# A hand-written order of steps, re-ordered: fused sparse attention and gated MLP on one core

## The chip, the cores and the metric

The kernel runs on one core of a Trainium2 chip. A core has five engines that run side by side: TensorE (PE, matmuls; PEld is its weight load), VectorE (DVE), ScalarE (ACT), GpSimd (POOL) and SyncE (SP, which here only starts transfers). The metric is the device time of one execution in microseconds (us), as the median of several runs.

## The reference, cut to what matters

There are 8 batches, 8 heads, 576 positions and 64 columns per head. The first half of the heads attends to the last 32 positions, the second half to the positions that are congruent modulo 32. The attention's output x then goes through a gated MLP.

```python
scores = scale * np.matmul(q, k.transpose(0, 1, 3, 2))
scores = np.where(masks, scores, -1e9); scores -= scores.max(-1, keepdims=True)
attn = np.exp(scores); attn /= attn.sum(-1, keepdims=True) + 1e-9
x = heads_to_columns(attn @ v)                 # (8, 576, 512)
h = gelu_tanh(x @ w_in)                        # 512 -> 1024
u, v = h[..., :512], h[..., 512:]
v_n = (v - mean(v)) / sqrt(var(v) + 1e-6) * g_ln
v_s = einsum('ts,bsd->btd', w_sg, v_n) + b_sg[None, :, None]
out = x + (u * v_s) @ w_out
```

## The kernel before

The loop runs over the 8 batches. While the MLP of batch b runs, the attention of batch b+1 is worked out beside it, and q, k and v of batch b+2 are loaded. Nothing is ordered by a scheduler at run time: three strings, START (batch 0 with the conversion of the weights), CYCLE (batches 1 to 6) and LAST (batch 7), list some hundred short steps, `emit` (L985) walks the list, and every engine and every DMA queue executes its instructions strictly in the order in which the list issues them. Only the order among steps of one engine matters; steps of different engines meet at semaphores and at buffers that come free.

A word is a step's name, an optional mark and an index: `ug:3` is the gelu of the fourth quarter of u. A trailing `-`, or none with a name in capitals, or `+`, names the batch of an attention step; `=` is a step without a batch. A `^` sets `alt`, which some helpers read: `loads()` (L144) puts a load on ACT's queue instead of SP's, `slow()` (L148) takes DVE instead of POOL, `fast()` (L152) POOL instead of DVE, and `mm_tile`/`at_tile` (L160, L163) swap the two PSUM pools, of two buffers of two banks each. Steps that read none of these ignore the mark.

The steps that matter here, by engine, for a batch in CYCLE:

- PE: `v1`, `v2`, `v` (x times the second half of w_in, 12, 12 and 8 matmuls), `u:0` to `u:3` (24 matmuls each, a PSUM tile each), `SL`, `SS` (scores), `s` (w_sg times the normed v, 28 matmuls a quarter), `PL`, `PS` (transposes of the softmax), `VA`, `PV`, `PW` (times v), `o`, `o2` (the two halves of the output product of a 128-row chunk, 6 matmuls each).
- ACT: `g` (gelu of v), `vh`, `ug` (gelu of u, which frees u's PSUM buffer), `lh` (normed v as high part), `EX` (exp), `sh` (gated product, high part), `XH`, `CL`, `CS` (copies), and the DMA issues `XD` (x to DRAM) and `od` (output). Gelu and exp lie in different activation tables, so an ACT_TABLE_LOAD is put between a gelu and an exp in ACT's order.
- DVE: `ls`, `lm`, `ll` (layer norm), `MK`, `MX`, `SU` (mask, max, sum of the softmax), `sm`, `sl` (gate, low part), `TQ` (transposes), `XL`, `XR`, `os`.
- POOL: `lr` (inverse square root by 14 tiny instructions), `SB`, `ML`.
- SP: loads `LQ`, `LP`, `LV`, `cl`, `wl`, `r`, `rt`.

In START the weights are converted by the chain `cl` (load), `ca`, `cb`, `cc`, `cd`, `ce`, `cf`, `cg`, `ch`, each by an index 0 to 15 over pieces of w_in and w_out; `ce` is one DVE instruction, and with `^` one on ACT and one on POOL. `TP` and `TC` turn the rows of q and k (PE) and copy them from PSUM (ACT).

Of the kernel before, what the change touches and what calls it, by code (L numbers as in the profile page):

```python
# [21 lines left out]


START = """
mk= mp= cl=:3 ca=:3 cl=:1 LP-^:3 cb=:3 cc=:3 ca=:1 cb=:1 cl=:0 cc=:1 cd=:1 cd=:3 cl=:2 TZ-:0
ca=:2 cl=:8 ml= ce=:3 ca=:0 cb=:0 ce=^:1 TP-^:6 TC-:6 cb=:2 TP-^:7 TC-:7 cf=^:1 cg=:1 cc=:2
cd=:2 LP-:0 SS-:3 LP-:1 TZ-:1 ca=:8 cb=:8 ch=:1 cc=:0 cd=:0 cl=:9 ce=^:0 TP-:1 MK-:3 TP-:0 TC-:0
MX-:3 SB-^:3 TC-:1 ce=:2 EX-:3 cf=^:2 LP-^:2 TP-^:2 TC-:2 SL-^:0 MK-:4 ca=:9 TP-^:3 TC-:3 SL-:1
MX-:4 wb= SB-:4 cl=:6 ca=:6 cb=:6 cc=:6 cl=^:4 cc=:8 LZ-:0 wc= wd= we= LZ-:1 wl=:1 MK-:5 MX-:5
cf=^:3 EX-:4 TP-:4 TC-:4 SU-:4 SB-:5 LP:1 SU-:3 cg=:2 ch=:2 cd=:8 TP-:5 cf=:0 wt=:1 TC-:5 SS-^:2  # L30
cd=:6 cg=:3 cl=^:7 EX-:5 ML-:4 SU-:5 TP^:2 TC:2 MK-:2 MX-:2 cg=:0 ch=:0 TZ:0 ce=^:6 LV-:0
ML-^:5 ca=:4 TP:3 TZ:1 TC:3 wh=:1 ch=:3 wm=:1 ca=:7 SB-^:2 PL-:4 CL-:4 PL-^:5 CL-:5 CM-:5 VX-:0
VY-:0 XR-:0 EX-:2 SU-:2 cb=:4 cc=:4 ML-^:2 LP:0 TP^:0 cb=:7 LV-:1 TC:0 XHa-:0 XLa-:0 ce=^:8
cf=:8 TP^:1 TC:1 cb=:9 cc=:9 XHb-:0 XLb-:0 cf=^:6 cl=:5 PS-^:2 CS-:2 ca=:5 XD-:0 SL^:0 SL:1 MK:0
VA-:1 XH-:1 XL-:1 cd=:4 cc=:7 LV-:2 PV-^:2 PW-:2 XH-:2 cd=:9 ce=:9 wo= wp= ML-:3 LP:2 XR-:1 MX:0
PS-:3 CS-:3 cb=:5 SB:0 XD-:1 va:0 vb:0 cl=^:13 TP^:4 TC:4 XL-:2 vc:0 LV-:3 PV-:3 XR-:2 PW-:3
cd=:7 XH-:3 cc=:5 TP^:5 EX:0 ce=:4 cf=^:4 cg=:4 ch=:4 va:1 XL-:3 xt LP:3 vd:0 g:0 XD-:2 vb:1
ce=:7 XR-:3 cf=^:9 ls:0 lr^:0 wl=:0 TP^:6 TC:6 cd=:5 cl=^:15 vc:1 cf=:7 cg=:7 cg=:9 vd:1 TP:7
v^:2 LZ:1 ce=:5 ch=^:9 ca=:13 cf=^:5 TC:7 cg=:6 g:1 LV:1 ls:1 cg=:5 ch=^:5 SS^:3 ch=:6 ch=:7 u:2
MK:3 TC:5 cb=:13 vh XD-:3 cc=:13 TZ+:0 cd=:13 ce=:13 lg= vl g:2 wt=^:0 cf=^:13 wl=^:4 rt cl=:10  # L40
lm:0 lh:0 ls:2 lm:1 wh=:0 lm:2 wm=:0 lr:1 lh:1 ll:0 cg=:8 SS:2 ug:2 lr:2 wl=:2 u^:1 ug:1 wt=^:4
ca=:15 ca=:10 cb=:10 cb=:15 u:0 SU:0 wh=:4 cc=:10 wl=:3 wm=:4 cc=:15 cd=:10 ce=:10 cf=:10 MK:2
wt=:2 LQ+:0 ug:0 wh=:2 wm=:2 cl=^:11 wt=^:3 wh=:3 wm=:3 ML:0 lh:2 ll:2 cg=:13 u:3 ll:1 cd=:15
ca=:11 ce=^:15 cb=:11 cc=:11 PL:0 CL:0 ch=:13 ug:3 MX:3 SB^:3 s:3 cd=:11 ce=:11 cf=:11 cg=:11
CM:0 s^:2 cf=^:15 MX:2 SB^:2 s^:0 ch=^:11 sm:3 sm:2 cl=^:12 ca=:12 TZ+:1 EX:3 SU:3 sh:2 sl:2 s:1
sh:3 cb=:12 ML^:3 LZ:0 cg=:10 cc=:12 VA^:1 cd=:12 LQ+:3 sm:0 ch=:8 cg=:15 cl=:14 ch=^:10 ca=:14
ch=^:15 ce=^:12 cf=:12 sh:0 sl^:0 TQ+:0 cg=:12 LV:0 sm:1 sh:1 sl:1 r cb=:14 cc=:14 EX:2 LQ+:1
VA:0 XR:1 PS:3 CS:3 o:0 o^:1 ch=:12 sl:3 cd=:14 ce=:14 cf=^:14 cg=:14 SU:2 ML^:2 XH:0 XL:0
ch=:14 XH:1 XL:1 LV:3 o^:2 o^:3 o2:2 os:2 XD:1 XR:0 XD:0 o2:0 o2:3 os:3 LV:2 PS^:2 o2:1 PV:3
PW:3 CS:2 od:2 PV:2 od:3 PW:2 TQ+:1 XH:3 LZ+:1 XL:3 XH:2 XR:3 XD:3 os:1 XR:2 XD:2 od:1 LZ+:0  # L50
os:0 od:0 LV+^:0 LQ+:2 LV+:1 XL:2
"""
# [16 lines left out]


# [971 lines left out]
```

## Time and profile before

| | |
|---|---|
| median of 3 runs (lowest, highest) | 584.68 us (584.05, 585.74) |
| the profiled execution | 583.31 us, of which 581.2 us are its span |
| busy: PE, PEld | 539.7 us (93%), 483.2 us (83%) |
| busy: DVE, ACT, POOL | 398.9 (69%), 250.1 (43%), 191.9 us (33%) |
| mean granted TensorE clock | 0.997 of full speed |

The span runs from the first to the last instruction of the profiled execution. Matmuls are pipelined and their ends are modelled, so a busy PE is one that has work under way; what it lacks to the span is time in which it waited.

### The profile page before, as it was taken

The page shows a single profiled execution, that of the slowest core. Times are in us where ns is not written, and L with a number is a line of the kernel's source. Part 1 is how long each engine was busy: PE and PEld are TensorE (multiplying, and loading weights), DVE is VectorE, ACT ScalarE, POOL GpSimd, SP SyncE. Part 2 cuts the span into 40 slices and gives each one's busy share as a digit, 9 for nine tenths or more (in the row PEclk, how much of TensorE's full clock was granted, in tenths as well). Part 3 has the DMA queues.
Part 4 walks back from the last instruction along what each step waited for, and adds up shares of the span by engine and source line. Part 5 has one row for each costly group of instructions (what it writes and reads, how often), then busy time and mean ns, then how long its engine had stood idle before and what let it go on. Part 6 is the DMA issues. An engine that isn't in the chain of part 4 may idle for free.

```text
span 581.2 us, 17089 instructions
## 1 busy us (share of the span) xinstructions
PE 539.7 (93%) x7217; PEld 483.2 (83%) x7217; DVE 398.9 (69%) x692; ACT 250.1 (43%) x371; POOL 191.9 (33%) x447
## 2 busy tenths in 40 slices
...
GB/s 242 179 191 188 128 136 106 180 156 148 184 50 42 185 154 123 42 118 176 173 50 47 184 158 122 42 120 179 172 53 47 186 186 4 1 122 157 1 0 90
DMA packets 253678, 70.08 MB, mean 121 GB/s; under 512 B 237793, under 2 KB 239329, under 8 KB 253602
## 3 DMA queue, kind: packets, MB, share of 16 engines
...
q8 instruction: 56, 0.92, 0.7%
...
## 4 chain that ended last, share of the span: by engine, by line
PE 72%; DVE 7%; POOL 7%; DMA 5%; ACT 5%; issue 3%; ACTq 1%; SPq 0%; POOLq 0%
PE sg L83 21%; PE o L83 17%; PE v L83 11%; PE u L83 10%; POOL nt L83 4%; PE ol L83 3%; PE os L83 3%; PE pts L83 2%; DMA xd<-xs 2%; POOL y L83 2%; PE ptl L83 1%; PE sa L83 1%; ACTq L83 1%; DMA stage<-in_moe_w_in_dram 1%; DVE bnst L83 1%
## 5 line engine op out<-in xcount | busy, mean ns | idle before, releaser
L83 PE MATMUL u<-xt,wih 128*128 128x288 f32 x512 | 105.6, 301 | 8.7 <-ACT u L83 8.3
L83 PE MATMUL sg<-wsh,vg 128*128 128x288 f32 x512 | 113.0, 296 | 0.0
L83 PE MATMUL o<-woh,vg 128*128 128x512 f32 x288 | 95.2, 397 | 0.0
L83 PEld LDWEIGHTS u<-xt,wih 128*128 128x128 f32 x512 | 83.2, 190 | 11.5 <-ACT u L83 9.7
L83 PEld LDWEIGHTS sg<-wsh,vg 128*128 128x128 f32 x512 | 85.6, 188 | 0.5
L83 PE MATMUL v<-wih,xt 128*128 128x512 f32 x256 | 83.9, 398 | 1.0 <-issue 1.0
L83 PE MATMUL u<-xt,wil 128*128 128x288 f32 x256 | 76.3, 298 | 0.8 <-DVE wil L83 0.8
L83 PE MATMUL sg<-wsl,vg 128*128 128x288 f32 x256 | 75.3, 294 | 0.0
L83 ACT ACT_TABLE_LOAD x40 | 51.3, 1283 | 54.9 <-DVE kT L83 23.2
L83 PEld LDWEIGHTS o<-woh,vg 128*128 128x128 f32 x288 | 54.1, 188 | 10.8
L83 PEld LDWEIGHTS v<-wih,xt 128*128 128x128 f32 x256 | 48.0, 188 | 12.2 <-issue 1.6
L83 PE MATMUL o<-wol,vg 128*128 128x512 f32 x144 | 56.3, 391 | 0.0
L83 DVE TENSOR_TENSOR ob<-o,xn 128x512 f32<-128x512 f32 x32 | 22.0, 689 | 45.1 <-PE o L83 44.3
L83 PE MATMUL v<-wil,xt 128*128 128x512 f32 x128 | 50.0, 391 | 0.0
L83 PEld LDWEIGHTS u<-xt,wil 128*128 128x128 f32 x256 | 48.7, 190 | 1.0 <-DVE wil L83 1.0
L83 ACT CAST vg<-gt 128x576 fp32r<-128x576 f32 (+2 forms) x48 | 22.8, 509 | 61.6 <-DVE gt L83 61.5
L83 PEld LDWEIGHTS sg<-wsl,vg 128*128 128x128 f32 x256 | 48.2, 188 | 0.0
L83 DVE TENSOR_TENSOR gt<-sg,u 128x576 f32<-128x576 f32 x32 | 23.6, 740 | 23.5 <-PE sg L83 14.6
L83 DVE BATCH_NORM_STATS2 bnst<-hv 128x6 f32<-128x512 f32 (+1 forms) x40 | 27.0, 676 | 17.4 <-ACT hv L83 17.1
L83 POOL TENSOR_TENSOR sms<-sms,sr 100x576 f32<-100x576 f32 x13 | 15.0, 1156 | 61.5 <-DVE sr L83 61.4
L83 DVE SCALAR_TENSOR_TENSOR vg<-hv,y,vg 128x512 fp32r<-128x512 f32 x32 | 22.5, 748 | 14.3 <-ACT vg L83 14.3
L83 ACT CAST xt<-ol 128x576 fp32r<-128x576 f32 (+2 forms) x17 | 10.3, 611 | 49.5 <-DVE ob L83 23.1
...
## 6 DMA issues: line engine op xcount, KB each, us to landing
xd<-xs ACTq DMA_DIRECT2D x128, 72.0 KB
...
```

What stands on the lines that cost most here:

```text
L83: ins = self.tc.keep_in_program_order(op(*args, **kwargs))
```

## The change

All three lists are written in a new order. Each holds the same steps as before (427, 139 and 72 of them). Some marks differ; those that have an effect are `ce=:1` (all on DVE), and in CYCLE `sl:2` and `ML:3` (now DVE), `CM:0` (now ACT), and the PSUM pools of `s:1` and `s:3`. A new helper `stores()` sends a store on SP's queue where the step is marked: that is `XD-:2` in START and `od:3` in CYCLE; the other `XD` and `od` stay on ACT's queue. START is cut here to its first lines and those around `XD-:2`.

```diff
@@ -22,49 +22,49 @@
 
 
 START = """
-mk= mp= cl=:3 ca=:3 cl=:1 LP-^:3 cb=:3 cc=:3 ca=:1 cb=:1 cl=:0 cc=:1 cd=:1 cd=:3 cl=:2 TZ-:0
-ca=:2 cl=:8 ml= ce=:3 ca=:0 cb=:0 ce=^:1 TP-^:6 TC-:6 cb=:2 TP-^:7 TC-:7 cf=^:1 cg=:1 cc=:2
-cd=:2 LP-:0 SS-:3 LP-:1 TZ-:1 ca=:8 cb=:8 ch=:1 cc=:0 cd=:0 cl=:9 ce=^:0 TP-:1 MK-:3 TP-:0 TC-:0
-MX-:3 SB-^:3 TC-:1 ce=:2 EX-:3 cf=^:2 LP-^:2 TP-^:2 TC-:2 SL-^:0 MK-:4 ca=:9 TP-^:3 TC-:3 SL-:1
-MX-:4 wb= SB-:4 cl=:6 ca=:6 cb=:6 cc=:6 cl=^:4 cc=:8 LZ-:0 wc= wd= we= LZ-:1 wl=:1 MK-:5 MX-:5
-cf=^:3 EX-:4 TP-:4 TC-:4 SU-:4 SB-:5 LP:1 SU-:3 cg=:2 ch=:2 cd=:8 TP-:5 cf=:0 wt=:1 TC-:5 SS-^:2
...
-cd=:7 XH-:3 cc=:5 TP^:5 EX:0 ce=:4 cf=^:4 cg=:4 ch=:4 va:1 XL-:3 xt LP:3 vd:0 g:0 XD-:2 vb:1
...
+mk= mp= cl=:3 ca=:3 LP-^:3 cb=:3 cc=^:3 cl=:1 ca=:1 cb=:1 TZ-:0 cc=:1 cd=:3 cd=:1 cl=:2 cl=:0
+ca=:2 ca=:0 cl=:8 ce=:1 TP-^:6 TP-^:7 cf=^:1 TC-^:6 ca=:8 cb=:2 cc=:2 TC-:7 SS-:3 cb=:0 ml=^
+cd=:2 cg=:1 LP-:0 LP-:1 ce=:3 cb=:8 ch=:1 cc=:0 MK-:3 cl=:9 cd=:0 ce=^:0 TP-:0 TC-:0 MX-:3 TP-:1
+TC-:1 TP-^:2 SL-^:0 LP-^:2 SB-^:3 ce=:2 TZ-:1 TC-:2 MK-:4 TP-^:3 ca=^:9 MX-:4 TC-:3 SL-:1 wb=
+SB-:4 cl=:6 ca=:6 LZ-:0 cb=:6 cf=^:2 cc=:6 EX-:3 cl=^:4 wc= cc=:8 cg=:2 wd= LZ-:1 wl=:1 MK-:5
+cf=^:3 EX-^:4 TP-:4 MX-:5 LP:1 SU-^:4 SU-:3 TP-:5 SB-:5 TP^:2 ch=:2 cd=:8 cg=:3 cf=:0 TC-:4
...
+vc:0 LV-:3 PV-:3 cc=:5 EX:0 PW-:3 XH-^:3 ce=:4 cf=^:4 va:1 XL-:3 xt cg=:4 vd:0 g:0 XD-^:2 XR-:3
+vb:1 ce=:7 LP:3 wl=^:0 cf=^:9 ls:0 TP:6 ch=:4 vc:1 cd=:5 ce=:5 LZ:1 cf=:7 cg=^:9 vd:1 ch=^:9
...
 """
 CYCLE = """
-xt r v1:0 SL:0 SL:1 MK:0 TQ:3 MX:0 SB^:0 v1:1 v2:1 g:1 ls:1 v2:0 rt g:0 ls:0 LQ+:0 lm:0 v^:2 vh
-vl u:2 ug:2 g:2 lr:1 EX:0 lr:0 lh:0 u^:3 ug:3 TQ:2 SS^:2 LQ+:1 lm:1 SS^:3 u^:0 ug:0 ls:2 lm:2
-lr:2 lh:2 ll:0 lh:1 MK:2 MX:2 SB:2 u^:1 EX:2 ll:2 ll:1 ug:1 s:1 s^:0 s^:3 TZ+:1 MK:3 TZ+:0 MX:3
-sm:1 SU:0 SB:3 EX:3 TQ+:0 sm:0 ML:0 s:2 sh:1 sh:0 sl:0 sm:3 sh:3 sl:3 LQ+:3 sl:1 SU:3 ML:3 o:0
-PL:0 sm:2 sh:2 sl^:2 o:1 o2:1 CL:0 CM:0 o:4 os:1 VA:0 VA:1 od:1 XH:0 SU:2 XL:0 ML:2 o2:4 XR:0
-os:4 od:4 o2:0 os:0 od:0 o:2 o2:2 os:2 PS^:2 XH:1 LV:2 PS:3 XL:1 o^:3 o2:3 XD:0 CS:2 XR:1 PV:2
-TQ+:1 LV:3 CS:3 PV^:3 PW:3 XD:1 XH:3 os:3 od:3 PW:2 XR:2 XH:2 XL:3 od:2 XD:2 XR:3 LZ+:1 LV+:1
-XD:3 LZ+:0 LV+:0 LQ+:2 XL:2
+v1:0 r SL:0 SL:1 TQ:3 v1:1 MK:0 xt MX:0 v2:1 SB^:0 g:1 ls^:1 v2:0 g:0 v^:2 vh lr:1 ls:0 u:2 ug:2
+u^:3 vl^ lm:0 g:2 TQ:2 lr:0 LQ+:0 lh:0 lm^:1 SS^:2 lh:1 SS^:3 ug:3 u^:0 ug:0 ls^:2 MK^:3 ll:1
+lr:2 TZ+:0 u^:1 ll:0 lm:2 lh:2 MK:2 ll^:2 MX:2 SB:2 ug:1 EX:0 SU^:0 MX:3 rt^ s^:1 s^:0 SB:3 s:3
+sm:0 TQ+^:0 EX:2 EX:3 sh:0 sl:0 sm:1 sm^:3 s:2 sh:3 ML:0 sl:3 sh:1 sl:1 SU:2 PL:0 LQ+:3 SU:3 o:0
+sm:2 TZ+:1 sh:2 sl:2 CL:0 o:1 LQ+:1 o2:1 CM^:0 ML:2 o:4 o2:4 VA:0 os:1 ML^:3 od:1 XR:0 VA:1 XH:0
+os:4 od:4 XD:0 XL:0 o2^:0 os:0 od:0 LV:2 o:2 o2:2 os:2 XH:1 PS:3 PS^:2 CS:2 o:3 TQ+:1 XR:1 o2^:3
+CS:3 LV:3 PV:2 PV^:3 XD:1 XL^:1 os^:3 PW:3 PW:2 XR:2 XH:3 XH:2 XL:3 LZ+:1 XD:2 XR:3 od^:3 XD:3
+LZ+:0 LV+:0 od:2 LV+:1 XL:2 LQ+:2
 """
 LAST = """
-v1:1 xt r v1:0 v2:0 g:0 v^:2 vh ls:0 lr:0 vl lm:0 g:2 ls:2 v2:1 u:3 g:1 u:0 lm:2 ug:3 ug:0 ls:1
-lm:1 lr^:2 lh:2 u^:2 u:1 lh:0 ll:0 lr:1 lh:1 ll:1 ug:1 ll:2 s:1 sm:1 sh:1 sl:1 s:0 sm:0 sh:0
-s^:3 sm:3 sh:3 sl:3 s:2 sl^:0 ug:2 o^:4 o:0 sm:2 sh:2 o:2 o^:3 sl:2 o2:3 os:3 od:3 o2:0 o2:2
-os:0 od:0 os:2 od:2 o:1 o2:1 o2:4 os:1 od:1 rt os:4 od:4
+v1:0 v2:0 xt g^:0 ls:0 v^:2 vh lr:0 v1^:1 vl v2:1 lm:0 g:2 ls^:2 g^:1 lh^:0 u:0 ls:1 ll:0 u^:3
+ug:3 lr^:2 lm:2 u^:1 lm:1 lr:1 lh:1 ll:1 lh:2 ug:0 ll:2 s^:1 u^:2 s^:0 ug:1 sm:1 r^ ug:2 sh:1
+sm:0 sl:1 s^:3 sm:3 sh:3 sl:3 s^:2 sm^:2 sh:0 sl^:0 o:2 sh:2 o:0 o^:3 sl:2 o2:3 o2:0 os:3 o2:2
+o^:4 o2:4 rt od:3 os:0 os:2 o:1 o2:1 od:2 os^:4 od:0 os^:1 od:4 od:1
 """
 
 
@@ -145,6 +145,10 @@
 
         return act if alt[0] else sp
 
+    def stores():
+
+        return sp if alt[0] else act
+
     def slow():
 
         return dve if alt[0] else pool
@@ -706,7 +710,7 @@
         dst = state[b, "xd"].rearrange("(n t) (h f d) -> h f t n d", t=32, h=NH, d=32)
         xs = state[b, "xs", hh].rearrange("p (n d) -> p n d", d=32)
         for f in range(4):
-            act.dma_start(dst[hh, f], xs[32 * f : 32 * f + 32])
+            stores().dma_start(dst[hh, f], xs[32 * f : 32 * f + 32])
 
     def strided_pt(b, hh):
         sm = sms[hh % 2][0:100]
@@ -947,10 +951,10 @@
     def out_send(b, kk):
         ob = state[b, "ob", kk]
         if kk < KF:
-            act.dma_start(out[b, kk * P : (kk + 1) * P, :], ob)
+            stores().dma_start(out[b, kk * P : (kk + 1) * P, :], ob)
         else:
             for i in range(2):
-                act.dma_start(out[b - 1 + i, KF * P : S, :], ob[TL * i : TL * i + TL])
+                stores().dma_start(out[b - 1 + i, KF * P : S, :], ob[TL * i : TL * i + TL])
 
     STEPS = {
 
```

The order by engine in CYCLE, where it differs most:

```
ACT before: g:1 g:0 vh ug:2 g:2 EX:0 lh:0 ug:3 ug:0 lh:2 lh:1 EX:2 ug:1 EX:3 sh:1 sh:0 sh:3 sh:2 ...
ACT after:  g:1 g:0 vh ug:2 g:2 lh:0 lh:1 ug:3 ug:0 lh:2 ug:1 EX:0 EX:2 EX:3 sh:0 sh:3 sh:1 sh:2 ...
DVE before: MK:0 TQ:3 MX:0 SB:0 ls:1 ls:0 lm:0 vl TQ:2 lm:1 ls:2 lm:2 ll:0 MK:2 MX:2 ll:2 ll:1 MK:3 MX:3 sm:1 SU:0 TQ+:0 sm:0 sl:0 sm:3 sl:3 sl:1 SU:3 sm:2 CM:0 os:1 SU:2 ...
DVE after:  TQ:3 MK:0 MX:0 SB:0 ls:1 ls:0 vl lm:0 TQ:2 lm:1 ls:2 MK:3 ll:1 ll:0 lm:2 MK:2 ll:2 MX:2 SU:0 MX:3 sm:0 TQ+:0 sl:0 sm:1 sm:3 sl:3 sl:1 SU:2 SU:3 sm:2 sl:2 os:1 ML:3 ...
PE: the same order but for PL:0 (now ahead of o:0), o2:4 (now ahead of VA:0) and PS:3 (now ahead of PS:2)
```

## Rows read from the trace of the kernel before

**Rows 1.** Stretches: length; busy PE, PEld, DVE, ACT, POOL (instructions); PE clock; DMA share; GB/s.
```profile
0.00:60.00 60.00, 36.37 (x746) 30.74 (x747) 44.90 (x89) 32.78 (x57) 28.01 (x49) 1.00 0.84 196
60.00:130.00 70.00, 67.74 (x913) 60.46 (x911) 61.47 (x123) 39.33 (x75) 28.55 (x51) 1.00 0.64 143
130.00:520.00 390.00, 379.12 (x5129) 340.89 (x5118) 267.18 (x430) 162.96 (x214) 124.83 (x317) 1.00 0.56 114
520.00:581.00 61.00, 56.46 (x452) 51.13 (x452) 25.38 (x52) 15.07 (x25) 10.47 (x31) 1.00 0.23 64
```

**Rows 2.** Waits of PE from 130 to 570 us: total, times, longest.
```profile
PE u L83 <- ACT u L83: 8.3, 6, 3.0
```

**Rows 3.** The chain that ended last, around u:1 of batch 5.
```profile
418.76 0.66 ACT u L83
419.46 3.46 PE u L83 x24
422.91 14.99 PE sg L83 x112
```

**Rows 4.** ACT in order of time, batch 5: start, us, instruction, idle before.
```profile
416.11 1.34 ACT L83 ACTIVATE vg<-hv,y 128x512 fp32r<-128x512 f32 x2 [1.55 <-POOL y L83]
417.46 1.28 ACT L83 ACT_TABLE_LOAD   x1
...
439.04 0.77 ACT L83 CAST vg<-gt 128x512 fp32r<-128x512 f32 x2 [3.26 <-DVE gt L83]
```

**Rows 5.** Groups of ACT instructions by shape: count, busy us, mean ns, idle before.
```profile
L83 ACT ACT_TABLE_LOAD x40 | 51.3, 1283 | 54.9 <-DVE kT L83 23.2 <-DMA xd<-xs 18.1 <-DMA v<-in_v_dram 12.3
```

**Rows 6.** POOL in order of time, batch 5, inside and at the end of lr:0.
```profile
415.11 0.68 POOL L83 TENSOR_SCALAR nt<-nt 128x2 f32<-128x2 f32 x1
415.88 0.19 POOL L83 TENSOR_TENSOR y<-nt,y 128x2 f32<-128x2 f32 x1
```

**Rows 7.** DVE in order of time, batch 5.
```profile
412.81 1.34 DVE L83 SCALAR_TENSOR_TENSOR hv<-hv,mv,g_bc 128x512 f32<-128x512 f32 x2
...
415.00 0.74 DVE L83 SCALAR_TENSOR_TENSOR hv<-hv,mv,g_bc 64x512 f32<-64x512 f32 x1
...
432.53 0.83 DVE L83 TENSOR_TENSOR vg<-gt,vg 128x512 fp32r<-128x512 f32 x2 [0.69 <-ACT vg L83]
...
437.15 0.75 DVE L83 TENSOR_REDUCE sr<-sms 100x16 f32<-100x576 f32 x1
...
438.31 0.69 DVE L83 TENSOR_TENSOR gt<-sg,u 128x576 f32<-128x576 f32 x1
```

**Rows 8.** The chain that ended last, batch 5, from the last s on.
```profile
437.90 1.39 PE o L83 x6
439.30 0.98 PE ptl L83 x9
```

**Rows 9.** PE in order of time, START: TP-:7 and SS-:3, waits behind.
```profile
11.04 1.22 PE L83 MATMUL turnk<-ident,rowk 96*128 96x96 f32 x6 [2.93 <-DMA rowk<-in_k_dram]
16.54 1.36 PE L83 MATMUL ss<-kT,qT 64*36 64x36 f32 x64 [4.27 <-ACT kT L83]
```

**Rows 10.** DVE in order of time, START: cf:1 behind ce:1.
```profile
16.03 0.69 DVE L83 TENSOR_TENSOR cv<-stage,cv 128x512 f32<-128x512 f32 x1 [2.51 <-POOL stage L83]
```

**Rows 11.** SP's queue in order of time: the issues around a gap.
```profile
16.75 0.33 SPq L83 DMA_DIRECT2D stage<-in_moe_w_in_dram  x1
23.05 0.30 SPq L83 DMA_DIRECT2D bst<-in_moe_b_sg_dram  x1
```

**Rows 12.** Stretches of START, columns as in rows 1.
```profile
17.00:23.00 6.00, 4.59 (x112) 4.23 (x110) 5.85 (x10) 3.75 (x7) 3.26 (x4) 1.00 0.59 155
...
27.00:40.00 13.00, 9.21 (x114) 7.36 (x106) 12.35 (x25) 9.19 (x18) 8.62 (x10) 1.00 0.99 208
```

**Rows 13.** The chain that ended last, batch 1: u:1.
```profile
157.05 4.98 PE u L83 x24
```

**Rows 14.** One microsecond of batch 1, columns as in rows 1.
```profile
158.00:159.00 1.00, 1.00 (x6) 1.00 (x5) 0.09 (x1) 0.66 (x2) 0.92 (x3) 0.50 0.88 142
```

More of the change, by code (lines that the diff above doesn't have):

```diff
@@ L31 @@
[L31 to L36, printed above, removed]
@@ L37 @@
-cd=:7 XH-:3 cc=:5 TP^:5 EX:0 ce=:4 cf=^:4 cg=:4 ch=:4 va:1 XL-:3 xt LP:3 vd:0 g:0 XD-:2 vb:1
[L38 to L48, printed above, removed]
@@ L49 @@
-ch=:14 XH:1 XL:1 LV:3 o^:2 o^:3 o2:2 os:2 XD:1 XR:0 XD:0 o2:0 o2:3 os:3 LV:2 PS^:2 o2:1 PV:3
-PW:3 CS:2 od:2 PV:2 od:3 PW:2 TQ+:1 XH:3 LZ+:1 XL:3 XH:2 XR:3 XD:3 os:1 XR:2 XD:2 od:1 LZ+:0
-os:0 od:0 LV+^:0 LQ+:2 LV+:1 XL:2
+mk= mp= cl=:3 ca=:3 LP-^:3 cb=:3 cc=^:3 cl=:1 ca=:1 cb=:1 TZ-:0 cc=:1 cd=:3 cd=:1 cl=:2 cl=:0
+ca=:2 ca=:0 cl=:8 ce=:1 TP-^:6 TP-^:7 cf=^:1 TC-^:6 ca=:8 cb=:2 cc=:2 TC-:7 SS-:3 cb=:0 ml=^
+cd=:2 cg=:1 LP-:0 LP-:1 ce=:3 cb=:8 ch=:1 cc=:0 MK-:3 cl=:9 cd=:0 ce=^:0 TP-:0 TC-:0 MX-:3 TP-:1
@@ new lines @@
+TC-:1 TP-^:2 SL-^:0 LP-^:2 SB-^:3 ce=:2 TZ-:1 TC-:2 MK-:4 TP-^:3 ca=^:9 MX-:4 TC-:3 SL-:1 wb=
+SB-:4 cl=:6 ca=:6 LZ-:0 cb=:6 cf=^:2 cc=:6 EX-:3 cl=^:4 wc= cc=:8 cg=:2 wd= LZ-:1 wl=:1 MK-:5
+cf=^:3 EX-^:4 TP-:4 MX-:5 LP:1 SU-^:4 SU-:3 TP-:5 SB-:5 TP^:2 ch=:2 cd=:8 cg=:3 cf=:0 TC-:4
+TC-:5 we=^ cd=:6 SS-^:2 cl=^:7 wt=:1 EX-:5 ML-:4 TC^:2 SU-^:5 MK-:2 cg=:0 TZ:0 ch=:0 ce=^:6
+ML-^:5 TP:3 ca=:4 TZ:1 MX-:2 ML-:3 wh=:1 TC:3 LV-:0 ca=:7 PL-:4 wm=:1 CL-^:4 cb=:4 PL-^:5 CL-:5
+SB-^:2 LP:0 CM-:5 ch=:3 VX-:0 VY-:0 EX-:2 XR-:0 LV-:1 SU-:2 ML-^:2 cb=:7 TP^:0 XHa-:0 XLa-:0
@@ new lines @@
+TC:0 cb=:9 ce=^:8 cf=:8 TP:1 TC:1 PS-^:2 XHb-:0 cc=:9 XLb-:0 cf=^:6 cc=:4 CS-:2 cl=:5 SL^:0
+ca=:5 SL:1 XD-:0 MK:0 VA-:1 XH-:1 XL-:1 cd=:4 cc=:7 LV-:2 PV-^:2 PW-:2 LP:2 cd=:9 XH-:2 ce=:9
+wo= cb=:5 XR-:1 MX:0 PS-:3 SB:0 wp= CS-:3 XL-:2 XD-:1 va:0 XR-:2 vb:0 cd=:7 cl=^:13 TP^:4 TC:4
+vc:0 LV-:3 PV-:3 cc=:5 EX:0 PW-:3 XH-^:3 ce=:4 cf=^:4 va:1 XL-:3 xt cg=:4 vd:0 g:0 XD-^:2 XR-:3
+vb:1 ce=:7 LP:3 wl=^:0 cf=^:9 ls:0 TP:6 ch=:4 vc:1 cd=:5 ce=:5 LZ:1 cf=:7 cg=^:9 vd:1 ch=^:9
+TP:7 lr^:0 v^:2 ca=^:13 TC:6 cg=:6 cf=^:5 g:1 TC:7 ls:1 cg=:7 cg=:5 cl=^:15 TP^:5 ch=:6 ch=^:5
```

12 lines of the change are left out of this document (added).

## The prediction

> **What bounds the kernel now.** I read the stretches of the span first, then PE's waits, then the chain that ended last, and only then single engines in order of time. The stretches [rows 1] show a kernel that is TensorE-bound for most of its length: from 130 to 520 us PE is busy 379.12 of 390 us, so all six CYCLE batches together can give back no more than 10.88 us. The last 61 us lack 4.54, most of it behind the last matmul (the final add and store), and from 60 to 130 us PE lacks 2.26. The first 60 us lack 23.63: there, PE waits for loads, weight conversion and the first softmax. A gain can come from two places only, the start and the waits inside CYCLE.
>
> In CYCLE one wait stands out: the matmuls of u wait for ACT's gelu of u, 8.3 us in 6 times, 3.0 the longest [rows 2], once a batch. The chain shows which: u:1 starts at 419.46, when ACT's gelu of u:3, begun at 418.76, has ended [rows 3], since u:1 takes u:3's PSUM buffer. Read backwards on ACT: lh:0 starts at 416.11 after waiting for POOL's y, its two instructions take 1.34 us, and a table load of 1.28 us follows at 417.46 [rows 4]. POOL's y is lr:0, which ends at 415.88 + 0.19 = 416.07 [rows 6]. So each batch stalls at u:1 behind lr:0, lh:0, a table load and ug:3, 0.7 us in the batch shown.
>
> **Fewer table loads.** The list of before switches tables six times a batch in CYCLE (gelu, exp, gelu, exp, gelu, exp), the new one twice. Four loads times six batches are 24 of the 40; at 1283 ns each [rows 5] this frees 30.8 us of ACT. Almost none of it is on a path, because ACT is busy 162.96 of 390 us in these batches [rows 1]. The one load on the path is that between lh:0 and ug:3, and the new order puts lh:1 exactly there. lh:1 has the same shape as lh:0 and takes about as long, 1.34 us for its two instructions against the load's 1.28 with the gap [rows 4]. Removing the loads by itself therefore gives nothing at u:1: what is gained by the load is spent on lh:1. I cost it at 0; bounds 0 and 1.28 a batch.
>
> The Trainium skill (ScalarE: Activation LUTs, section What ACT_TABLE_LOAD costs) puts a switch at 2.66 us, 1.28 for the load and 1.38 for a drain. Here ACT's lh:0 ends at 417.45 and the next gelu begins at 418.76, so the switch took 1.31 and no such drain shows [rows 3, 4]. By the page the new order would take 1.38 us more off u:1's wait where that much is left, and the sum below would be 4.4 us lower; by the rows it is not.
>
> **lr:0 ends earlier.** What does shorten the path is on DVE and POOL. While DVE runs a two-input instruction of the layer norm, POOL's tiny instructions stretch: the one at 415.11 took 0.68 us beside lm:2 (415.00, 0.74 us), where its like takes 0.19 [rows 6, 7]. The new DVE order moves lm:2 from ahead of ll:0 to behind ll:1 and ll:0, out of lr:0's time; lm:1 (two instructions from 412.81) stays in it. lr:0 ends 0.68 - 0.19 = 0.49 earlier; vl ahead of lm:0 pushes a little of lm:0's stretch into lr:0's window, so I take 0.45. lh:0, lh:1, ug:3 and u:1 move with it. Six batches: 2.7 us. Below, 0 if another stretch takes its place; above, the 8.3 us.
>
> **What is pushed later.** lm:2 behind ll:1 and ll:0 delays lh:2 and ll:2, which s:1 needs at its 13th matmul. ll:1 follows lh:1's first half, four instructions of the ll and lm kind at 0.7 us follow each other, then lm:2 (0.74), MK:2 and ll:2: by these durations ll:2 ends about 423.6. s:1 starts at 422.3 and needs it 12 matmuls later, at 423.9 (14.99 us for 112 of them [rows 3]). Hidden, by 0.3 us.
>
> EX:0, EX:2 and EX:3 move behind ug:1 and ahead of sh:0. Their users are far (PL:0 comes after the last s), and EX:3, behind ug:1, a table load, EX:0, SU:0, MX:3 and SB:3, ends by the same walk at about 430.2, before sh:0 can start at 430.8. Hidden, by 0.6.
>
> SU:2 and SU:3 now both stand before sm:2 on DVE. SU:3 alone ran from 437.15 to sm:2's start at 438.31, 1.16 us [rows 7]. With sm:0 at 430.05 (s:0's end and 0.3), two transposes of TQ at about sm's 0.69 each, sl:0 (0.83), sm:1, sm:3 behind s:3's end, a wait of 0.7 for sh:3, sl:3 and sl:1 (0.83 each), then two times 1.16, sm:2 starts at 439.1; sh:2 (0.77) [rows 4] and the first part of sl:2 bring its data to 441.15. PE, which runs PL:0 (0.98), o:0 and o:1 (1.39 each) [rows 8] from 437.2 on, reads it first at 441.4. Hidden, by 0.2: this is the thinnest cover of the change, and any lateness on DVE beyond it is paid six times.
>
> CM:0 on ACT, sl:2 and ML:3 on DVE instead of POOL, TQ:3 ahead of MK:0 and the swapped PE steps fill time in which these engines wait; 0. od:3 on SP's queue takes one issue off ACT, which then waits for PE anyway; LV behind it on SP waits for PW, later than od:3 does; 0.
>
> **START.** Now SS-:3 waits 4.27 us for TC-:7's copy, and starts at 16.54 [rows 9], because cb:0 and ce:1's ACT half stand ahead of it; DVE stands 2.51 us until 16.03 for ce:1's POOL half [rows 10]. The new list puts both copies ahead of cb:0 and ce:1 on DVE alone (0.69 us more there, by the shape of rows 10). TC-:7 then follows the turn of k (11.04 to 12.3 [rows 9]) and cb:2 at about 12.9, so that SS-:3 can start near 13.7, some 3 us earlier, and DVE, on which the start depends (44.90 busy of 60 us, and 12.35 of 13 between 27 and 40 [rows 1, 12]), begins its dense stretch at about 13.2 instead of 16.0: 2.8 - 0.7 = 2.1. SP's gap from 17.1 to 23.05 [rows 11] closes by about as much, so the loads behind it come earlier too. Against it: DMA is 0.99 busy from 27 to 40 us [rows 12] and may hold the chain. XD-:2 on SP puts four sends, which wait for XR-:2, ahead of LP:3; TP:6 reads LP:3 some 5 us later, covered by little. Bounds: 3.9 us (every wait of the walk gone) and -1 (TP:6 late, DMA holding the rest). I take 2.0.
>
> LAST has no PE wait to win between 520 and the last matmul; its s:1 comes after three u instead of four, with about 0.5 us cover. 0.
>
> **Sum.** 583.31 (the profiled execution: span 581.2 and 2.1 around it) - 2.0 - 2.7 = 578.6. The median of the runs stands 1.37 above the profiled execution, so I forecast **580.0**.
>
> **Rivals.**
> (1) *Only CYCLE gains.* START is held by DMA, as the 0.99 speaks for; the first loads, free until 27 us at 0.59 from 17 to 23 [rows 12], speak against. 584.7 - 2.7 = 582.0.
> (2) *More.* START gives 3.9, and batch 1's stall of 3.0 shortens enough that the clock holds: behind it, PE ran at 0.50, the lower level of 1.2 GHz [rows 14], and u:1 took 4.98 us where 3.46 is usual [rows 3, 13]. 584.7 - 3.9 - 2.7 - 1.5 = 576.6. The stall I expect (2.6) is nearer to 3.0 than to those of the other five, (8.3 - 3.0) / 5 = 1.1 on average, behind which the clock held (0.997 over the whole span, in the table above), so I left this out.
> (3) *Nothing.* lr:0 is stretched by ll or lm at other places, START's earlier copies wait for the next load: 584.7.
> (4) *Slower.* DVE, with SU:2, SU:3, ML:3 and sl:2 more between the last s and o2:1, delivers sl:2 late. At 1.0 us later than worked out, six stalls of 0.8 us eat the whole gain; at 1.7 later, 9.0 - 4.7 gives 589. For it speaks the cover of 0.2; against it, that DVE waits 0.7 us for sh:3 inside that walk, which absorbs lateness from before.
> (5) *u:1's wait goes wholly.* A switch of tables holds ACT for longer than its rows show, so that without it ug:3 comes as much earlier as PE can use: 1.8 us in batch 1 and the whole stall in the others, 7.1 of the 8.3 us [rows 2]; 584.7 - 2.0 - 7.1 = 575.6. Against it speaks the 1.31 us from lh:0's end to ug:3 [rows 3, 4]. This is what the drain of the page on ScalarE in the Trainium skill would make of it.
>
> **How the numbers follow.** The forecast has 0.48 (its own range 578 to 582), (1) 0.14, (2) 0.11, (3) 0.11, (4) 0.14, (5) 0.02. A change under 0.3%, 1.75 us, cannot be told from none here. Faster: nearly all of the forecast, (2), (5) and most of (1), 0.68; same: (3) and the edges of (1) and (4), 0.18; slower 0.14. The range goes from 576.0, below (2), to 585.5, leaving out (5) and most of (4).
>
> **What would show it.** In the trace of after: 16 table loads instead of 40; SS-:3 starting near 13.7 us; PE's lack in the first 60 us down by 2; u:1's waits down from 8.3 to about 5.6 in sum, 0.3 in batch 5, with lh:1 directly ahead of ug:3; no new PE wait of o for the low part of the gate. A PE wait at o2:1 or at TP:6, or u:1's wait unchanged, would make it wrong.

## The result, and the profile of the changed kernel

The changed kernel takes 578.96 us (median of 10 runs, 577.29 to 583.05), the kernel before 585.29 in the same measurement (10 runs, 581.88 to 587.19): a ratio of 0.9902, with a 95% interval of 0.9874 to 0.9931, so 5.7 us less (4.0 to 7.4). The forecast was 580.0, in a range of 576.0 to 585.5. The profiled execution of the changed kernel took 579.7 us, its span 577.5.

The stretches of the changed kernel, with the columns of [rows 1]:

```profile
0.00:60.00 60.00, 39.93 (x801) 33.54 (x802) 50.30 (x93) 33.62 (x59) 25.64 (x48) 0.97 0.85 199
60.00:130.00 70.00, 67.00 (x832) 58.67 (x824) 62.64 (x120) 37.32 (x72) 27.12 (x50) 1.00 0.61 141
130.00:520.00 390.00, 382.24 (x5300) 343.50 (x5283) 278.73 (x442) 130.98 (x198) 116.64 (x302) 1.00 0.55 115
520.00:577.00 57.00, 53.48 (x321) 48.18 (x319) 23.67 (x50) 14.09 (x24) 11.19 (x31) 1.00 0.22 60
```

TensorE is 3.56 us busier in the first 60 us than in [rows 1] and 3.12 us busier in the CYCLE stretch, and slightly less busy from 60 to 130. But busy time isn't work: the clock of the first stretch is 0.97, and a matmul at the lower clock is busy for longer. So I also compare when a fixed piece of work starts, the first v matmul of each batch, read from TensorE's timelines (us):

```
batch     0       1       2       3       4       5       6       7
before  56.26  126.26  197.80  262.04  328.68  392.61  458.79  522.42
after   53.62  126.71  196.91  260.76  326.51  389.55  455.28  518.83
lead     2.64   -0.45    0.89    1.28    2.17    3.06    3.51    3.59
```

In this pair of executions START's lead of 2.6 us is gone by batch 1, and the 3.6 us at the end were all won in batches 1 to 6. The experiments show that this is one draw: TensorE's clock differs from execution to execution.

The waits of TensorE from 130 to 566 us (total, times, longest), beside [rows 2]:

```profile
PE u L83 <- ACT u L83: 6.9, 5, 3.4
PE sg L83 <- DVE t L83: 0.4, 1, 0.4
PE ss L83 <- DVE kT L83: 0.4, 1, 0.4
PE ol L83 <- issue: 0.3, 1, 0.3
```

The wait of u:1 fell from 8.3 to 6.9, and its longest, in batch 1, grew from 3.0 to 3.4. Three waits that the first trace also had are gone: 1.03 us of batch 1's strided scores for kT, 0.40 of its u for hv, and six times 0.23 ahead of PV:3, which I had not taken into account. As forecast, 16 table loads are left (group of ScalarE, count, busy, mean ns, idle before):

```profile
L83 ACT ACT_TABLE_LOAD x16 | 20.5, 1283 | 46.7 <-DMA v<-in_v_dram 18.5
```

### The profile page after: what moved, and what is told of

It is laid out like the page before. It is cut to its first block, busy times and chain, and to the rows that moved or that the text cites. A ratio compares the mean times of both kernels' runs of the same rounds, so it can differ in the third digit from the quotient of the medians.

```text
span 577.5 us, 17028 instructions
## 1 busy us (share of the span) xinstructions
PE 542.7 (94%) x7217; PEld 483.9 (84%) x7217; DVE 415.3 (72%) x702; ACT 216.0 (37%) x352; POOL 180.6 (31%) x431
## 5 line engine op out<-in xcount | busy, mean ns | idle before, releaser
L83 DVE TENSOR_TENSOR gt<-sg,u 128x576 f32<-128x576 f32 x32 | 23.8, 743 | 23.3 <-PE sg L83 20.7
L83 POOL MEMSET v<- 32x128 f32 x16 | 3.1, 198 | 97.9 <-PE os L83 70.6
L83 ACT ACTIVATE vg<-hv,y 128x512 fp32r<-128x512 f32 x32 | 20.7, 712 | 33.6 <-POOL y L83 31.6
L83 DVE TENSOR_TENSOR vg<-gt,vg 128x576 fp32r<-128x576 f32 (+2 forms) x45 | 23.2, 554 | 12.1 <-ACT vg L83 12.1
```

The costliest lines, as they stand in the source:

```text
L83: ins = self.tc.keep_in_program_order(op(*args, **kwargs))
```

## The experiments

**E1 to E3: one list at a time.** The kernel before with START, CYCLE or LAST exchanged for the new list, the other two left alone.

> The kernel before with START of the new lists alone; CYCLE and LAST as before. Theory A (the one of the prediction, START worth 2.0 us): 585.3 - 2.0 = 583.3 us, and the lead of the first matmul of v (53.6 us against 56.3) is still there when batch 1's first v matmul starts (before 126.3, then about 124). Theory B (from the trace of the changed kernel, where batch 1's v starts at 126.7): the lead is used up between 71 and 126 us, because TensorE then comes earlier to the w_sg and w_in conversions of VectorE and waits there; nothing is left at the end: 585.3 us, at most 0.5 away.

> The kernel before with CYCLE of the new lists alone; START and LAST as before. Theory A (prediction): 2.7 us less, 582.6. Theory B (trace of after): CYCLE brings nearly the whole gain, 4 us or somewhat more, 581 us: u:1's waits go from 8.3 to about 6.5 in sum, the six waits of 0.23 ahead of the strided P V matmuls go (1.4), and batch 1's waits of 0.40 (u for hv) and 1.03 (ss for kT) go or stay according to whether they belong to START (then 582.5).

> The kernel before with LAST of the new lists alone. Theory A (prediction, LAST worth 0): 585.3 us. Theory B (trace of after): the tail behind the last matmul is 0.9 us shorter, and a wait of 0.4 us at s:1 for the low part of layer norm's last rows comes in: 584.8 us. A third, since the profiled execution of after fell 3.6 us and the medians 6.3: LAST brings 2 us or more, 583.

START alone: 580.40 us, ratio 0.9927 (0.9901 to 0.9953), 4.3 us less. CYCLE alone: 583.57, 0.9971 (0.9944 to 0.9998), 1.7 less. LAST alone: 584.96, 0.9987 (0.9965 to 1.001). Theory B, which I had formed on two profiles, falls in E1 and E2: START brings most of the gain, and CYCLE not the 4 us that it had there but about what the prediction had. LAST brings little or nothing; 2.1 us or more is out. Part of why one pair of traces misled shows in TensorE's clock. Stretches of E1, of E3 (which has START as before) and of the changed kernel: length, busy TensorE, its clock, DMA share, GB/s.

```profile
20.00:60.00 40.00, 31.61 (x682) 1.00 0.77 176
150.00:170.00 20.00, 17.91 (x135) 1.00 0.48 76
```
```profile
20.00:60.00 40.00, 29.07 (x645) 0.63 0.74 171
150.00:170.00 20.00, 15.77 (x224) 0.91 0.60 118
```
```profile
20.00:60.00 40.00, 31.86 (x674) 0.96 0.78 175
150.00:170.00 20.00, 16.60 (x114) 0.91 0.47 75
```

With either list the clock falls to its lower level of 1.2 GHz for a part of 20 to 60 us in some executions and stays at 2.4 GHz in others. All profiles, by their START (E6 and E8 have one mark of the new one off):

```
START   kernel   clock 20-60   first v of batch 1   u:1's wait in batch 1   clock 150-170
before  before      1.00            126.26               3.0              0.91
before  E2          0.59            128.81               3.4              0.91
before  E3          0.63            128.95               3.3              0.91
before  E9          1.00 (*)        128.24               2.5              0.91
before  E10         0.75            128.11               3.3              0.91
before  E12         1.00            125.66               3.0              0.91
copies  E5          0.74            126.65               3.3              0.91
new     after       0.96            126.71               3.4              0.91
new     E1          1.00            124.32               2.1              1.00
new     E4          0.91            128.00               1.8 (at s:1)     1.00
new     E6          1.00            124.88               1.4              1.00
new     E7          0.74            128.59               none             1.00
new     E8          1.00 (*)        131.02               none             1.00
new     E11         1.00            125.66               4.1              0.91
```

(*) In E8 and E9 the row of the granted clock misses a fall. Two v matmuls in E6, then in E8, then in E2 (whose clock fell there by its row too):

```profile
53.75 0.61 PE L82 MATMUL v<-wih,xt 128*128 128x512 f32 x2
```
```profile
57.43 1.05 PE L82 MATMUL v<-wih,xt 128*128 128x512 f32 x2
```
```profile
56.88 1.05 PE L83 MATMUL v<-wih,xt 128*128 128x512 f32 x2
```

Where the clock held, START brings the first v matmul of batch 0 forward by 2.4 us on average (56.26 and 55.70 against 53.14, 53.29 and 54.39 in E1, E6 and E11), near the 2.0 of the forecast, but that of batch 1 by only 1.0 (126.26 and 125.66 against 124.32, 124.88 and 125.66), and the two groups touch. Where it fell, no clear lead is left at batch 1. The rest of its 4.3 us lies in batch 1, which takes 67.8 us in E1, from its first v matmul to that of batch 2, and 70.4 to 71.5 in the six profiles with START as before. E1 has none of the waits for kT (0.7 to 1.0 us in those six), its u:1 waits 2.1 us, and the clock stays up. The 0.40 us wait for hv is in the profile of before alone, so it isn't START's.

The last two columns tell what hangs on u:1's wait: in batch 1 the clock fell behind each wait of 2.5 us or more and behind none of 2.1 or less. The length of the wait alone doesn't decide it: in batch 4 the clock is 0.91 from 350 to 370 us in E12 and E11, behind waits of 1.8 and 2.2 us.

**E4: ug:3 ahead of lh:0.**

```diff
-u^:3 vl^ lm:0 g:2 TQ:2 lr:0 LQ+:0 lh:0 lm^:1 SS^:2 lh:1 SS^:3 ug:3 u^:0 ug:0
+u^:3 vl^ lm:0 g:2 TQ:2 lr:0 LQ+:0 ug:3 lh:0 lm^:1 SS^:2 lh:1 SS^:3 u^:0 ug:0
```

> The changed kernel with one step moved: ScalarE's gelu of u:3 ahead of lh:0 in CYCLE, so that it doesn't stand behind POOL's lr:0. Theory C (u:1's wait is nothing but ug:3's place in ScalarE's queue behind lr:0 and lh): the waits of u:1, 6.9 us in sum, go wholly; s:1 then comes earlier and waits for ll:2, whose cover was 0.27 us in batches 2 to 6 and 1.7 in batch 1 (ll:2 ended at 292.12, s:1 read it at 292.39), so that about 1.1, 0.4, 0.4, 0 and 0.5 us come back in batches 2 to 6 and 1.7 in batch 1: a net gain of 2.8 us, and 1 to 1.5 more if the clock holds in batch 1: 575 to 576 us. Rival: ug:3 ahead of lh:0 delays the whole of the layer norm by its 0.65 us and s:1 by as much; the gain is 0 to 1 us, 578 to 579.

577.50 us, ratio to before 0.9856 (0.9819 to 0.9894): 8.4 us below the kernel before where the changed kernel is 5.7 below, a net 2.7; by the medians the net is 1.5, and the two intervals overlap. Expected were 2.8, and 1 to 1.5 more if the clock held in batch 1, which it did: the 575 to 576 us were missed. The traces show the mechanism: no wait of u:1 is left, and in its place stand those of s:1 for ll:2. From the waits of TensorE (the sixth, of 0.4 us, is in LAST):

```profile
PE sg L83 <- DVE t L83: 5.3, 6, 1.8
```

In E4's batch 3, lr:2 on POOL (start, us; its first, one of its stretched and its last instruction), and VectorE's ll:1 and ll:0:

```profile
283.18 0.22 POOL L83 TENSOR_SCALAR va<-mv 64x1 f32<-64x1 f32 x1 [0.29 <-DVE mv L83]
...
285.07 0.71 POOL L83 TENSOR_TENSOR nt<-nt,va 64x1 f32<-64x1 f32 x1
...
288.78 0.18 POOL L83 TENSOR_TENSOR y<-nt,y 64x1 f32<-64x1 f32 x1
```
```profile
284.98 2.74 DVE L83 SCALAR_TENSOR_TENSOR vg<-hv,y,vg 128x512 fp32r<-128x512 f32 x4 [0.47 <-ACT vg L83]
```

Fourteen tiny instructions take 5.8 us; those beside VectorE's ll take 0.57 to 0.71 us each, the others 0.18 to 0.22. That is the next thing on the path.

**E5: the two copies of START.** The kernel before with one stretch of START reordered:

```diff
-ca=:2 cl=:8 ml= ce=:3 ca=:0 cb=:0 ce=^:1 TP-^:6 TC-:6 cb=:2 TP-^:7 TC-:7 cf=^:1 cg=:1 cc=:2
+ca=:2 cl=:8 ml= ca=:0 ce=:1 TP-^:6 TC-:6 cb=:2 TP-^:7 TC-:7 cb=:0 cf=^:1 ce=:3 cg=:1 cc=:2
```

> The kernel before; in START only, ce:1 on VectorE alone and cb:0 and ce:3 behind TC-:6 and TC-:7, so that the two copies that SS-:3 needs come first. Theory A (the prediction's account of START: the copies are what it is worth): SS-:3 starts at about 13.5 us instead of 16.5, the first matmul of v 2 us or more earlier, and the time is 2 to 4 us below 585.1, as in START alone (580.4). Rival: the work behind them (loads, softmax, other conversions) holds the rest at its old times, and less than 1 us arrives: above 584.

583.35 us, ratio 0.9961 (0.9941 to 0.9981): 2.3 us less, half of what START brings. SS-:3 starts at 13.94, and against E2, E3, E9 and E10, whose clock fell too, batch 1's first v comes 1.5 to 2.3 us earlier. Its strided scores still wait 0.92 us for kT: that wait belongs to another part of START.

**E6: five loads of v on SP.** The changed kernel with `LV+^:0` near the end of START as `LV+:0`.

> The changed kernel with one mark off: the five loads of v for batch 2's first heads at the end of START issued by SP instead of ScalarE. Theory D (batch 1's long wait of u:1, 3.4 us, and the clock behind it come from ScalarE issuing 14 transfers until 138.2 us, before it gets to gelu g:1, whose matmuls had ended near 137.5): ScalarE is free at about 133.8, g:1 starts near the end of its matmuls, about 2 us earlier against v1:0, the wait in batch 1 shrinks to about 1.5 us and the clock holds there: 2 to 3.5 us below 578.96. Rival: the loads then stand on SP's queue ahead of q and k of batch 2 and delay TQ:2, so that the strided scores wait instead: within 0.5 us of 578.96.

574.79 us, ratio to before 0.9832 (0.9799 to 0.9866), 4.1 us more than the change gains, and more than the 2 to 3.5 expected. ScalarE in order of time at the end of START, in the changed kernel and in E6 (ACTq is its queue of transfers):

```profile
132.73 1.01 ACTq L83 DMA_DIRECT2D out_dram<-ob  x2
133.79 4.35 ACTq L83 DMA_DIRECT2D v<-in_v_dram  x5
138.17 1.28 ACT L83 ACT_TABLE_LOAD   x1 [10.69 <-DMA rawq<-in_q_dram]
139.47 1.94 ACT L83 ACTIVATE hv<-v 128x1024 f32<-128x1024 f32 x2
```
```profile
131.56 1.35 ACTq L82 DMA_DIRECT2D out_dram<-ob  x2
132.94 1.28 ACT L82 ACT_TABLE_LOAD   x1 [7.29 <-DMA xd<-xs]
135.40 1.03 ACT L82 ACTIVATE hv<-v 128x1024 f32<-128x1024 f32 x1 [1.17 <-PE v L82]
```

In the changed kernel g:1 comes late because ScalarE is still issuing (15 transfers from 127.5 us on); in E6 it waits 1.17 us for its matmuls. Batch 1's wait falls from 3.4 to 1.4, as worked out, and the clock holds there.

**E7 and E8: the layer norm's chain, and all together.** E7 is E4 with these steps moved (E8 is E7 with E6's edit):

```diff
-ls^:2 MK^:3 ll:1 lr:2 TZ+:0 u^:1 ll:0 lm:2 lh:2 MK:2 ll^:2 MX:2 SB:2 ug:1 EX:0 SU^:0 MX:3 rt^
+ls^:2 lm:2 lr^:2 ll:1 TZ+:0 u^:1 ll:0 lh:2 ll^:2 MK^:3 MK:2 MX:2 MX:3 SB:2 ug:1 EX:0 SU^:0 rt^
```

> E4 and, in CYCLE too, lm:2 and lr:2 on VectorE right behind ls:2, then ll:1, ll:0, lh:2, ll:2, and MK:3, MK:2, MX:2, MX:3 behind these. Theory C goes on: in E4 the waits for the low part of the layer norm's last rows (1.80, 1.32, 0.54, 0.64, 0.64 us in batches 1, 2, 4, 5, 6) come from lr:2 on POOL, which took 5.8 us beside VectorE's ll where its like takes 3.8 for twice the columns; with lr:2 on VectorE (11 instructions of about 0.19, 2.1 us) ll:2 ends 1.5 us earlier, and those waits go but for part of batch 1's: 3 to 4 us below E4's 577.5, so 573.5 to 574.5. Rival: the 2.1 us on VectorE push MX:3, SB:3 and EX:3 behind sh:0's time (cover 0.6 us) and o2:1 or PL:0 waits: no gain over E4.

> E6 and E7 together. If both hold, TensorE has hardly a wait left between 100 and 540 us: about 571 to 572.5 us, less than either alone; if batch 1's wait is one and the same in both, the gain of E6 counts only once: 573.

E7: 572.87 us, ratio to before 0.9785 (0.9749 to 0.9821), somewhat below the 573.5 to 574.5 expected. E8: 571.93, 0.9760 (0.9721 to 0.9799): 7.0 us below the changed kernel, but not to be told from E7, so that the two gains add is not shown. VectorE in E7, batch 3, and the CYCLE stretch with the columns of [rows 1]:

```profile
283.35 0.14 DVE L83 TENSOR_SCALAR va<-mv 64x1 f32<-64x1 f32 x1
...
285.27 0.15 DVE L83 SCALAR_TENSOR_TENSOR y<-nt,y 64x1 f32<-64x1 f32 x1
285.34 2.73 DVE L83 SCALAR_TENSOR_TENSOR vg<-hv,y,vg 128x512 fp32r<-128x512 f32 x4
288.10 0.75 DVE L83 SCALAR_TENSOR_TENSOR t<-hv,y,t 64x512 fp32r<-64x512 f32 x1
```
```profile
130.00:520.00 390.00, 386.50 (x5341) 346.63 (x5340) 294.52 (x514) 132.82 (x198) 91.07 (x219) 1.00 0.56 117
```

lr:2 takes 2.07 us here. TensorE lacks 3.5 us of 390, where it lacked 10.88 before and 7.76 after the change.

**E9: lm:2 alone.** The kernel before; lm:2 and lh:2 behind ll:0:

```diff
-ls:2 lm:2 lr:2 lh:2 ll:0 lh:1
+ls:2 lr:2 ll:0 lm:2 lh:2 lh:1
```

> The kernel before; in CYCLE only lm:2 (and with it lh:2) behind ll:0, out of lr:0's time. Theory A (the prediction's step: lm:2 stretches one of lr:0's instructions by 0.49 us, and nothing else changes): the stretched instruction near lr:0's end goes, lr:0 takes 4.9 to 5.2 us instead of 5.4 to 5.7, and the waits of u:1 in batches 2 to 6 fall from 5.0 to 5.3 in sum to about 2.8. Rival (the stretch moves): VectorE then starts something else there, lr:0 keeps its length, and the waits stay at 4.2 or more.

One run, 584.62 us, beside 585.73 of before. lr:0 takes 4.5 to 5.5 us, 5.2 on average of batches 2 to 6 (before 5.4 to 6.0, 5.6 on average), and the stretch at its end is gone. In batch 5 another one has taken its place: the 0.68 of [rows 6] is 0.20 now, but one instruction takes 1.87 us beside lm:1, and lr:0 is no shorter (5.48 us, before 5.42). POOL:

```profile
413.36 1.87 POOL L83 TENSOR_TENSOR nt<-y 128x2 f32<-128x2 f32 x1
...
416.98 0.20 POOL L83 TENSOR_TENSOR y<-nt,y 128x2 f32<-128x2 f32 x1
```

The waits of u:1 fall to 3.6 us in batches 2 to 6 (0.53, 1.07, 0.64, 0.80, 0.53; before 5.3), below the 4.2 to 6.1 of the other profiles with this order of ScalarE and VectorE but not to the 2.8 expected: the step is real in part. The distance of the batches doesn't shrink, though: from u:1 of batch 1 to that of batch 6 it is 328.99 us (before 328.51), because lh:1 and ll:1 now come later: the 112 matmuls of s in batch 5 take 15.5 us from first start to last end, before 15.15, and as much longer in each of batches 2 to 6.

**E10 and E12: the wait of 0.23 us.** The kernel before, in E10 with PS:3 ahead of PS:2, in E12 with XD:0 ahead of od:0.

> The kernel before; in CYCLE only PS:3 ahead of PS:2, as in the new list. In the kernel before TensorE waits 0.23 us ahead of PV:3 in each of six batches, 1.4 in sum; in the changed one it doesn't. Theory E: the order of the two transposes does it (it sets which PSUM tile PV:3 takes, and so that it waits for VectorE's os:3, which ends 0.11 us before PV:3 starts): with the swap alone the six waits go. Rival: LV:3's load lands late, because it was issued 3.40 us ahead of PV:2 where the changed kernel issues it 4.03 ahead: then the swap alone leaves the waits.

> The kernel before; in CYCLE only XD:0 ahead of od:0 on ScalarE, as in the new list. E10 left the 0.23 us ahead of PV:3 in place. In the trace of before the second load of LV:3 is issued at 386.77, 2.3 us after od:0's output was sent (384.15), and in the changed kernel at 383.52; in the program's order that load is the eighth transfer behind od:0 in the first and behind a send of XD:0 in the second, and the program has a load wait for the transfer eight issues before it. Theory G: the load is late for that reason, lands after PV:2, and that is the 0.23 us; with XD:0 ahead of od:0 it is issued some 3 us earlier and the six waits go (1.4 us). Rival: the load isn't what PV:3 waits for; its issue moves and the waits stay.

One run each: 584.61 us (before 585.73) and 581.60 (before 586.30); single runs of the kernel before lie up to 7.5 us apart, so the traces are read and not the times. In E10 the six waits stay, in E12 they are gone. TensorE and VectorE's os:3 in E10, then the same in E12:

```profile
390.34 0.67 PE L83 MATMUL os<-pts,v 36*64 36x36 f32 x32
391.24 0.45 PE L83 MATMUL os<-pts,v 36*64 36x36 f32 x17 [0.23 <-issue]
```
```profile
390.45 0.69 DVE L83 TENSOR_TENSOR ob<-o,xn 128x512 f32<-128x512 f32 x1 [0.77 <-PE o L83]
```
```profile
389.88 2.07 PE L83 MATMUL os<-pts,v 36*64 36x36 f32 x128
```
```profile
389.99 0.69 DVE L83 TENSOR_TENSOR ob<-o,xn 128x512 f32<-128x512 f32 x1 [0.54 <-PE o L83]
```

In E10 TensorE goes on at 391.24, 0.10 us after os:3 ends at 391.14; in E12 it runs through while os:3 works, to 390.68. So my theory G has the right edit and the wrong reason: the second load of LV:3 is issued 3.59 us ahead of PV:2 in E12, hardly more than before (3.40). In the traces of before and of E10, PV:3 carries a wait for VectorE and the next v1:0 carries none; in E12 and in the changed kernel it is the other way round. By this PV:3 takes another PSUM buffer. Why the place of a send decides which buffer that is stays open.

**E11: an exp put back.** The changed kernel with EX:0 ahead of lh:0.

> The changed kernel; in CYCLE only EX:0 back ahead of lh:0, so that two table loads come back in each batch and one of them stands between lh:1 and ug:3. By the rows (a switch took 1.31 us): u:1's waits grow by 1.3 us in each batch, from 0.7 to 2.0 in batches 3, 4 and 6, and to above 4 in batch 1; about 8 us in sum, 586 to 588. By the drain that the Trainium skill's page on ScalarE adds (2.66 us for a switch; ScalarE: Activation LUTs, What ACT_TABLE_LOAD costs): 2.7 us in each, 16 us in sum. Rival: no growth, since EX:0 finds ScalarE waiting for y and its loads hide there: 579.

One run, 586.89 us. ScalarE in batch 3, in the changed kernel and in E11:

```profile
284.35 2.56 ACT L83 ACTIVATE vg<-hv,y 128x512 fp32r<-128x512 f32 x4 [4.19 <-POOL y L83]
286.81 1.16 ACT L83 ACTIVATE u<-u 128x576 f32<-128x576 f32 x2
```
```profile
284.31 2.57 ACT L83 ACTIVATE vg<-hv,y 128x512 fp32r<-128x512 f32 x4 [1.73 <-POOL y L83]
286.89 1.28 ACT L83 ACT_TABLE_LOAD   x1
288.19 1.19 ACT L83 ACTIVATE u<-u 128x576 f32<-128x576 f32 x2
```

Counted from lh:0's start, ug:3 starts 1.42 us later behind the load (3.88 against 2.46), 1.31 us after lh:1's end, and u:1's waits grow from 6.9 to 13.1 us, 1.0 on average (expected 1.3). The switch costs what the rows said. The Trainium skill (ScalarE: Activation LUTs, What ACT_TABLE_LOAD costs) has 2.66 us for it, which would have been 16 us in sum by that estimate; the measurement decides.

## Why the prediction was right, and which of its steps were not

That the sum came out 1 us from the measured time is in part luck. Alone, START brings 2.3 us more than forecast and CYCLE 1.0 less, and by the traces 1.4 of what CYCLE brings come from a wait that the sum did not have.

**START: the term was mis-sized.** The forecast took 2.0 us; START alone brings 4.3 (2.7 to 5.8), which leaves no room for rivals (1) and (3). The mechanism held as far as it went: SS-:3 starts at 13.45 us (forecast 13.7), TensorE lacks 3.5 us less in the first 60 in E1, where the clock held (forecast 2), and the copies alone are worth 2.3. What failed is that the working stopped at 60 us. More than half of the lead at the first v matmul of batch 0 is lost by batch 1, and then about 3 us are won in batch 1, where the prediction had put nothing for START. The loss is not the wait for VectorE's weight conversion that theory B of E1 named. TensorE has such waits in the changed kernel, and in the kernel before they have the same sum:

```profile
74.40 0.40 PE L83 MATMUL u<-xt,wil 128*128 128x288 f32 x1 [1.01 <-DVE wil L83]
...
87.62 0.74 PE L83 MATMUL wsgT<-ident,wsg 128*128 128x128 f32 x5 [0.74 <-PE wsgT L83]
...
93.36 0.37 PE L83 MATMUL sg<-wsh,vg 128*128 128x288 f32 x1 [0.49 <-DVE wst L83]
```
```profile
75.70 0.40 PE L83 MATMUL u<-xt,wil 128*128 128x288 f32 x1 [0.81 <-DVE wil L83]
...
84.85 0.49 PE L83 MATMUL wsgT<-ident,wsg 64*128 64x64 f32 x5 [1.16 <-DVE wst L83]
...
89.54 0.74 PE L83 MATMUL wsgT<-ident,wsg 128*128 128x128 f32 x5 [0.28 <-PE wsgT L83]
```

Where it is lost stays open, and so does which of START's other moves shortens batch 1: none was tried alone. (More marks have an effect than the section on the change lists: in START `wl=^:0`, now on ScalarE's queue, and the PSUM pools of `TP:1` and `TP:6`; in LAST the pools of six steps.) The risk that I named, the sends of XD-:2 ahead of LP:3 on SP, showed where the clock held: TP:6 waits 0.72 us for its rows in E6 and 0.42 in E11, and not at all in the profile of the changed kernel.

**u:1's wait: the step on lr:0 failed.** I forecast 8.3 to 5.6 and it became 6.9. lr:0 did lose its stretch: it takes 4.8 us on average of batches 2 to 6, before 5.6. But vl and lm:0 had changed places, and lm:0 now holds up lr:1, which runs just ahead of lr:0 on POOL and grew from 4.54 to 5.41 us in batch 5, and by as much in the others. The two cancel: counted from the first v matmul of its batch, lr:0 ends at 23.7 us on average of batches 2 to 6, before at 23.8, where the sum had 0.45 earlier. POOL and VectorE in the changed kernel, batch 5:

```profile
405.84 1.79 POOL L83 TENSOR_TENSOR nt<-y 128x2 f32<-128x2 f32 x1
```
```profile
406.17 1.39 DVE L83 SCALAR_TENSOR_TENSOR hv<-hv,mv,g_bc 128x512 f32<-128x512 f32 x2
```

I had put "a little" of lm:0 in lr:0's window and never looked at lr:1's. In batch 1 the same order makes lr:1 7.0 us long instead of 4.5, and with START alike u:1 waits 3.4 us where E1, with the list as before, waits 2.1: this is the cost of the new CYCLE that START's gain covers. Most of the fall that is left comes from the step that I had put at 0: lh:1 in the place of the table load is shorter by 0.19 us in each batch (ug:3 starts 2.46 us after lh:0's start, before 2.65). In batch 5 a wait of 0.36 us for kT has taken the place of u:1's 0.73.

**CYCLE as a whole.** Forecast 2.7, measured alone 1.7 (0.1 to 3.3). The waits in the trace of the changed kernel sum to somewhat more, 1.4 from u:1 and 1.4 from the wait ahead of PV:3, which E12 traces to one send moved on ScalarE. I had no step for that second wait at all.

**The covers held.** ll:2 ends 0.24 us ahead of s:1's need in batches 2 to 6 (forecast 0.3), E4 shows what it costs once that is gone, and no wait came in at sh:0 or o2:1. The slower rival, sl:2 late, did not happen. Of rival (2) START's larger gain came true, but not the clock: in batch 1 the new START holds it with the old CYCLE (E1), and the change as a whole doesn't. Rival (5) is refuted by E11.

**LAST:** forecast 0, measured 0.8 less with an interval across 0. In the traces the last matmul ends 0.8 us later after batch 7's first v, 0.38 of it a new wait at s:1, and the tail behind it is 0.9 us shorter.
